# Fewer, wider products of zeros in the opening, and the second half of each pair's outputs 1.5 steps later: a gated recurrence with a squared-ReLU FFN

## The chip, the core and the metric

The kernel runs on one core of a Trainium2 chip. The core has five engines that run side by side, each with its own queue of instructions: TensorE (PE, the matrix products; its weight loads are shown as PEld), VectorE (DVE), ScalarE (ACT), GpSimd (POOL) and SyncE (SP, which here issues the transfers). Products land in eight accumulation banks (PSUM), from which DVE and ACT read them. The metric is the device time of one launch in microseconds (us); a listed time is one execution.

## The reference

A gated recurrence over 768 positions is computed for 4 batches and 8 heads of 48 elements, and its output, 3072 tokens of 384 elements, goes through a feed-forward layer with 2048 hidden elements and a squared ReLU. All of it is float32.

```python
for t in range(S):                       # S = 768
    state = alpha[:, :, t, :, None] * state + np.einsum('bhd,bhe->bhde', k[:, :, t], v[:, :, t])
    y[:, :, t] = np.einsum('bhd,bhde->bhe', q[:, :, t], state)
x = y.transpose(0, 2, 1, 3).reshape(B * S, H * D)
h = np.maximum(x @ w_in, 0.0)            # 384 -> 2048
return h * h @ w_out                     # 2048 -> 384
```

## The kernel before

*The recurrence in blocks.* The sequence is cut into 6 chunks of 128 positions; a chunk of one batch is a block, 24 in all, numbered so that four neighbours are the four batches of one chunk. A block goes through: logarithm of alpha (`ln`), running sums of it by a product with a triangle of ones (`cs`, lines 283 to 287), their exponentials (`eb`, `ei`), scaled q and k and their transposes (`turn`, tile T, line 578), and then, on PE, `scores` (line 413) and `state_sums` (line 442), both into tiles called sckv, and the outputs y (line 393). DVE takes the masked scores from the bank (`masked`, tile am) and the sums (`sums_copied`, tile us), and then makes the next state s (`next_state`).

*Pairs.* Blocks are taken in pairs. `ga` (line 502) does scores, state sums and their DVE work for a block n of the next pair, and the first half of the products of y for the pair a before: those with the state, and the inner ones on the diagonal. `gb` (line 524) does the rest of y, 32 small inner products, and then the scores, state sums and DVE work of block n + 1. After `gb` the outputs are ready: 12 copies (`ev`, line 616) bring y from its two banks to x, the input of the FFN; they run on ACT, apart from a few named in `evd`. The two banks of y are drawn in `ga` and are free once these copies have read them.

*The FFN.* Tokens are taken in six groups of four blocks. Group 0 multiplies in plain float32. From group 1 on, operands are split in parts, and three products stand for one: with parts (xa, wb), (xl, wl) and (xd, wd) in the first layer, line 726, 128x512 each, three matmuls per part; with (ha or hx), hl, hd and wb, wl, wd in the second, line 809, 128x384. ACT and DVE finish the h tiles (lines 741 to 767: `hid`, `h`), split them (lines 701 and 653) and add the parts (line 648). Group 1 still does a part of the second layer as plain products (o<-w_out,hid).

*One ring of banks.* `ps_att` and `ps_ffn` are one pool with eight banks, drawn in turn: h, o, cs, T, sckv, y, warm and zeros all draw from it, and a draw waits until the last readers of the bank drawn eight draws ago have ended.

*Who sets the order.* The program order is written by hand through the table `AT`. The opening is a list of words, `AT['first']`, each of which calls one step (line 977); among them are `warm0`, `zeros4` and `zeros1`, products of zeros whose results nobody reads: they keep PE at work while data are under way. Three more (`warm`, line 236) stand ahead of the list. After the opening, `layer_in` and `layer_out` give the units of the FFN with costs in units of about 1.2 us (an `in_x` is 1.05, an `out_x` 1.08, an `out_plain` 1), and `attention` gives events with a time on the same scale; `weave` (line 1051) puts each event ahead of the first unit whose time is not less than the event's. `attention` takes `ga` and `gb` at `t + AT['ga']` and `t + AT['gb']` where its scale is 1: that is in group 1 (for the pair that starts block 10, at t = 13, and the pair that starts block 12, at t = 35.25) and in groups 2, 3 and 4 (`AT['g']`: t = 2.075 and 14.25). With the event `gb` go the four steps of the copies (`ev_part`, at 0.1 apart) and the loads of v for the next pair and one of k, issued by SP. The splits of x for the next group stand at 51.0 (group 1) and 48.75 (the others).

The events of `attention` that matter here:

```python
w = t + (AT[f] if scale == 1 and f in ("ga", "gb") else at) * scale
...
elif f == "gb":
    if whole_at is None:
        out.append((w, gb, given))
    if after:
        for p in range(NP):
            out.append((w + AT["evs" if scale == 1 else "evs0"] * p, ev_part, (old, p)))
```

The functions that the change touches, and what calls them:

Of the kernel before, what the change touches and what calls it, by code (L numbers as in the profile page):

```python
# [9 lines left out]
FP32 = mybir.dt.float32  # L10
# [8 lines left out]


GB = 4
AT = {'thrp': 4.5, 'cvo': 3.35, 'thr': 2.25, 'm48': 16, 'cvs': 3.9, 'cv1': 0.125, 'later': (0, 0, 4, 6, 0, 1, 0), 'evs': 0.1, 'lead': 4, 'post': 3, 'w_first': (46.0, 38.0, 49.0), 'wstep': 1.0, 'w_in_at': 2.5, 'w_in_by': 3.6, 'room1': 22, 'room': 24, 's0': 4, 'ahead': 6, 'late': 2, 'xs': 0.0, 'g0': ((0.5, 4, False, True, 27.75), (25.75, 6, True, True), (29.25, 8, True, False)), 'sc0': (3.25, 2.35, 2.35), 'g1': ((5.5, 8, False, 15.0), (13.0, 10, True), (35.25, 12, True)), 'g': ((2.075, 6, True), (14.25, 8, True)), 'g1x': 51.0, 'gx': 48.75, 'g0x': 56.25, 'k0': 2, 'h0': 15, 'k1': 4, 'h1': 3, 'h1by': 2, 'evs0': 0.7, 'tp': 'ADMD', 'tp1': 'ADAD', 'split': 8, 'o0': (46.5, 48.5), 'o1': (), 'o2': (21.25, 24.75, 24.5, 40.0, 35.25, 28.25), 'str1': 21.5, 'ga': 9.75, 'gb': 12.5, 'cv0': -1.25, 'pre': '1a 0a 0q 0k 1k 1q', 'cp': ('q2a', 'k2b', 'k0a', 'k3a', 'k3b', 'k0b', 'q0b', 'q3b', 'q2b', 'q3a'), 'evd': ((0, 0, 0), (0, 0, 1), (0, 1, 2), (0, 1, 3), (2, 0, 3), (2, 1, 1), (2, 1, 2)), 'first': 'ln0 load1v cs0 ei0 eb0 zeros4 mk0 mq0 qT0 kT0 ln1 cs1 kc0 ei1 warm0 load0v eb1 mk1 qc0 weights0 lt1 sc0 load2a mq1 load2q kT1 kc1 qT1 load2k load3a qc1 load3k kv0 am0 first0 load3v sc1 ln2 kv1 load3q us0 am1 weights6 us1 cs2 ya0 ei2 second0 eb2 lt0 ln3 yb0 load2v mq2 qT2 mk2 load4a ep00 ep01 qc2 kT2 cs3 kc2 eb3 ei3 zeros1 sc2 ep02 mq3 mk3 kT3 ep03 weights2 first1 st0 ha0 second1 lt2 kv2 am2 qT3 load4k kc3 qc3 ha1 weights5 first2 sc3 kv3 am3 load4q us2 ha2 us3 ya2 yb2 weights3 ep20 ep21 ep22 load4v ep23 second2 first3 weights1 st1 weights4 ha3 lt3 hb0 st2 second3 hb2 hb3 hb1 st3'}


RUN = {0: 128, 32: 32, 64: 64, 96: 32}
# [3 lines left out]
def kernel(  # L29
# [12 lines left out]
    nc = tc.nc  # L42
# [3 lines left out]
    NP = H // 2  # L46
# [12 lines left out]
    ps_att = ctx.enter_context(tc.tile_pool(name="ps_att", bufs=8, space=PSUM))  # L59
# [11 lines left out]
    s_t = [s_all.pop(0) for _ in range(B)]  # L71
# [36 lines left out]
    def move(us, out, in_):  # L108
        ins = nc.sync.dma_start(out=out, in_=in_).ins
        ahead = 0.0  # L110
        for before, took in reversed(under_way):
            if ahead >= AT["thrp" if us == 1.0 else "thr"]:
                tc.add_manual_dep(
# [16 lines left out]
    def load(n, xs="aqkv"):  # L130
        c, b = divmod(n, B)
        for x in xs:
            t = tile_of(x, n)
            if id(t) in owner:
                need(("free", *owner[id(t)]))
            owner[id(t)] = x, n
            given.add((x, n))
            move(
                1.1,
                out=t[:, :, 0:D] if x in "qk" else t.rearrange("a (h d) -> a h d", h=H),  # L140
                in_=srcs[x][b, :, c * C : (c + 1) * C, :].rearrange("h s d -> s h d"),
            )
# [3 lines left out]
    def load_weights(i):  # L146
        src, k = (moe_w_in, KM) if i < NW else (moe_w_out, NJ // NW)
        p = i % NW * DF // NW
        src = src[:, p : p + DF // NW] if i < NW else src[p : p + DF // NW, :]
        if src.dtype == FP32:  # L150
            raws[i] = to = target(i)
            src = src.rearrange("(k r) f -> r k f", r=128)
        else:
            src = src.bitcast(U16).rearrange("(k r) f -> r k f", r=128)[:, :, 1:]
            raws[i] = raw_pool.tile([128, k, src.shape[2] + 1], U16, tag="raw", name="raw")
            to = raws[i][:, :, :-1]
        move(2.3, out=to, in_=src)
# [42 lines left out]

    for word in AT["pre"].split():
        load(int(word[0]), word[1:])
# [30 lines left out]
    nc.vector.memset(rebias, -8.0 * 14336.0)  # L233


    def warm(_):
        nc.tensor.matmul(
            out=ps_att.tile([128, NP, 64], FP32, tag="att", name="warm"),
            lhsT=s_t[0].rearrange("a p d -> a (p d)")[:, 0:128], rhs=s_t[0], start=True, stop=True,
        )  # L240

    for _ in range(3):
        warm(0)


    blk = [{} for _ in range(NBLK)]
# [4 lines left out]
    def bank(n, name, shape=(NP, C)):  # L251

        return ps_att.tile([128, *shape], FP32, tag="att", name=name)

    def work(name, bufs=1):
        return p2.tile([128, NP, C], FP32, tag=name, name=name, bufs=bufs)
# [7 lines left out]

    SPLIT = AT["split"]

# [98 lines left out]
    def copied(x, n):  # L365
        t = blk[n][f"{x}s"] = work(f"{x}s", 2 if x == "k" else 4)
        copy = nc.vector.tensor_copy if f"{x}{n}" in AT["cp"] else nc.scalar.copy
        copy(out=t, in_=blk[n].pop(f"{x}T"))
# [4 lines left out]
    def kc(n):  # L373
        (copied if n < GB else turned_copied)("k", n)


    def zeros(n):

        ps = bank(n, "zeros", (2 * NP, 64))
        for _ in range(n):  # L380
            nc.tensor.matmul(
                out=ps[:, 0 : NP // 2, :], lhsT=s_t[3].rearrange("a p d -> a (p d)")[:, 0:128],
                rhs=s_t[3][:, 0 : NP // 2], start=True, stop=True,
            )

    def y_begin(n):
        ys, seen = [bank(n, "y", (2, NP // 2, C)) for _ in range(2)], set()
# [45 lines left out]
    def state_sums(n):  # L433
        need(("v", n), ("kb", n))
        given.add(("free", "k", n))
        ps = two[n]
        m = D if n >= AT["m48"] else 64
        for p in range(NP):
# [25 lines left out]
    def rows_of(n):  # L464
        return [slice(0, D), slice(64, 64 + D)] if n >= AT["m48"] else [slice(0, 128)]

# [174 lines left out]
    here, todo, room = {}, [], [22]  # L641
# [8 lines left out]
    late = [False]  # L650
# [303 lines left out]
    steps = {f.__name__: f for f in (ln, sp, cs, eb, ei, mq, mk, bl, br, lt, qT, qc, kT, kc, ev)}  # L954
# [2 lines left out]
    steps["ya"], steps["yb"] = lambda n: ga(n, None), lambda n: gb(n, None)  # L957
    steps["load"] = load
    steps["weights"] = lambda _: load_weights(to_load.pop(0))
    steps["warm"] = warm  # L960

    def ep(n, p):
        need(*[("xp", n, i) for i in range(p)])
# [1 line left out]
        ev(n, (p,))  # L965

    steps["ep"] = ep
    steps["zeros"] = zeros

    def half_in(x, j):  # L970
        given.add(("h" + x, j))
# [5 lines left out]
    first = AT["first"]  # L977
# [129 lines left out]
    cv0 = AT["cv0"]  # L1107
    cvs = AT["cvs"]
# [17 lines left out]
    for g in range(1, NG):  # L1126
# [11 lines left out]
        if g == 1:  # L1138
# [5 lines left out]
            n = min(AT["k0"], AT["k1"])  # L1144
# [34 lines left out]
```

## Time and profile before

| | |
|---|---|
| three runs | 518.58, 518.98, 520.09 us (median 518.98) |
| span of the profiled execution | 518.6 us (its own listed time isn't given apart from these runs) |
| PE busy | 507.8 us, 5338 matmuls and as many weight loads |
| PE idle after 37 us | 1.1 us at 239 us and 0.1 at 271 us |
| DVE, ACT, POOL busy | 355.7, 306.4, 5.3 us |
| stretch 0 to 37 us | PE busy 30.9 us, DVE 20.6, ACT 24.7 |
| stretch 37 to 126 us | PE busy 88.96 us of 89.0 |
| stretch 214 to 295 us | PE busy 79.8 us of 81.0 |
| granted clock in the records | 1.00 in every stretch |
| DMA moved | 102.3 MB, 197 GB/s over the span |

The stretches are time from the span's start: the opening up to 37 us, then group 0 (to 126 us), group 1 (to 214), group 2 (to 295), group 3 (to 374), group 4 (to 449) and group 5. A busy PE is one whose records cover the time; the records of matmuls that follow each other overlap a little. What an engine waited for is inferred from semaphore events, and "issue" stands for no visible releaser. A product in float32 whose operands are not split takes two passes and appears as two matmuls.

### The profile page before, as it was taken

Reading aid. Unit: us, or ns where it says so; the run is one execution under the profiler, and the core shown is the slowest. Engines: PE = TensorE matmul, PEld = TensorE weight load, DVE = VectorE, ACT = ScalarE, POOL = GpSimd, SP = SyncE. Lnnn points to the kernel's source line nnn. Section 1 sums busy time; section 2 is a strip of 40 time slices with the busy share of each in tenths; the row PEclk is TensorE's granted clock in tenths of the full one; section 3 lists DMA queues with packets and bytes.
Section 4 is the critical chain, followed back from the end, with each engine's and each line's share of the span. In section 5 each row is a group of like instructions: output and inputs, shape, how many; then the busy total and the mean of one; then the engine's idle time right before and its main releaser. Section 6 shows DMA issues by size and latency. Waiting matters only on the chain.

```text
span 518.6 us, 13019 instructions
## 1 busy us (share of the span) xinstructions
PE 507.8 (98%) x5338; PEld 418.9 (81%) x5338; DVE 355.7 (69%) x628; ACT 306.4 (59%) x649; POOL 5.3 (1%) x29
## 2 busy tenths in 40 slices
PE   7899999999999999999999999999999999999997
PEld 5675455678888669987899988899988899988997
DVE  2766669986887877776697468587465487363861
ACT  4788898547888653485664276772275673164620
POOL 4000000000000000000000000000000000000000
PEclk9999999999999999999999999999999999999999
DMA  9999779472777786898884688864683545699201
GB/s 183 204 267 237 197 189 235 93 228 80 238 190 184 246 243 162 265 279 227 205 225 143 222 247 222 223 200 152 213 274 124 185 121 154 207 380 322 65 2 61
DMA packets 139323, 102.34 MB, mean 197 GB/s; under 512 B 109808, under 2 KB 115968, under 8 KB 139264
## 3 DMA queue, kind: packets, MB, share of 16 engines
q1 hardware_dynamic: 139264, 101.51, 68.2%
q8 instruction: 42, 0.69, 0.6%
q14 instruction: 17, 0.14, 0.1%
HBM read 84.16 MB, written 17.33 MB: 196 GB/s over the span
## 4 chain that ended last, share of the span: by engine, by line
PE 93%; DVE 4%; issue 1%; POOL 1%; ACT 1%; DVEq 0%; POOLq 0%
PE o L809 39%; PE h L726 32%; PE h L919 8%; PE y L393 4%; PE sckv L413 2%; PE T L578 2%; PE sckv L442 2%; PE cs L283 1%; PE cs L286 1%; DVE x L616 1%; PE cs L287 1%; DVE hd L648 1%; DVE hx L653 0%; DVE am L424 0%; ACT x L616 0%
## 5 line engine op out<-in xcount | busy, mean ns | idle before, releaser
L726 PE MATMUL h<-xd,wd 128*128 128x512 f32 x240 | 68.1, 396 | 1.1 <-issue 1.1
L726 PE MATMUL h<-xa,wb 128*128 128x512 f32 x240 | 68.7, 394 | 0.0
L726 PE MATMUL h<-xl,wl 128*128 128x512 f32 x240 | 67.9, 391 | 0.0
L648 DVE TENSOR_TENSOR hid<-h,hid 128x512 f32<-128x512 f32 x40 | 27.6, 689 | 51.1 <-PE h L726 51.0
L616 ACT COPY x<-y 48x256 f32<-48x256 f32 (+3 forms) x133 | 46.7, 365 | 21.2 <-PE y L393 18.8
L809 PE MATMUL o<-wb,ha 128*128 128x384 f32 x160 | 54.5, 340 | 0.0
L743 ACT ACTIVATE h<-h 128x512 f32<-128x512 f32 x40 | 23.3, 582 | 52.3 <-PE h L726 52.3
L809 PE MATMUL o<-wl,hl 128*128 128x384 f32 x160 | 53.7, 336 | 0.1
L809 PE MATMUL o<-wd,hd 128*128 128x384 f32 x304 | 53.7, 334 | 0.0
L809 PE MATMUL o<-w_out,hid 128*128 128x384 f32 x160 | 53.6, 489 | 0.0
L726 PEld LDWEIGHTS h<-xl,wl 128*128 128x128 f32 x240 | 45.1, 188 | 10.1 <-DVE xl L653 0.4
L809 PEld LDWEIGHTS o<-wd,hd 128*128 128x128 f32 x304 | 52.8, 188 | 0.0
L726 PEld LDWEIGHTS h<-xa,wb 128*128 128x128 f32 x240 | 44.4, 188 | 9.8 <-ACT hid L763 0.4
L726 PEld LDWEIGHTS h<-xd,wd 128*128 128x128 f32 x240 | 44.0, 188 | 9.1
L809 PE MATMUL o<-wb,hx 128*128 128x384 f32 x144 | 48.3, 336 | 0.0
L809 PE MATMUL o<-wl,hx 128*128 128x384 f32 x144 | 48.1, 334 | 0.0
L809 PEld LDWEIGHTS o<-w_out,hid 128*128 128x128 f32 x160 | 30.0, 190 | 19.7
L741 ACT ACTIVATE hid<-h 128x512 f32<-128x512 f32 x40 | 24.2, 606 | 32.9 <-PE h L726 32.5
L919 PE MATMUL h<-x,w_in 128*128 128x512 f32 (+1 forms) x120 | 43.4, 512 | 0.2 <-DVE x L616 0.2
L701 ACT ACTIVATE ha<-hid 128x512 fp32r<-128x512 f32 x40 | 25.1, 642 | 20.3 <-PE o L809 7.9
L919 PEld LDWEIGHTS h<-x,w_in 128*128 128x128 f32 x120 | 22.1, 190 | 17.8 <-issue 15.3
L653 DVE SCALAR_TENSOR_TENSOR hl<-ha,hid 128x512 fp32r<-128x512 f32 x40 | 27.5, 687 | 6.9 <-ACT ha L701 6.8
(111 smaller groups left out, 852.5 us busy)
## 6 DMA issues: line engine op xcount, KB each, us to landing
wd<-do SPq DMA_DIRECT2D x36, 384.0 KB
wl<-lo SPq DMA_DIRECT2D x34, 384.0 KB
wl<-li SPq DMA_DIRECT2D x32, 384.0 KB
wd<-di SPq DMA_DIRECT2D x32, 384.0 KB
raw<-in_moe_w_out_dram SPq DMA_DIRECT2D x8, 767.5 KB
raw<-in_moe_w_in_dram SPq DMA_DIRECT2D x8, 767.2 KB
v_in<-in_v_dram SPq DMA_DIRECT2D x24, 192.0 KB
out_dram<-osb SPq DMA_DIRECT2D x24, 192.0 KB
```

The lines of the kernel that those rows point to most:

```text
L393: ins = nc.tensor.matmul(out=ys[e][64 * half : 64 * half + D + G * e, m % 2, p // 2, t], lhsT=lhsT, rhs=rhs, start=(half, e) not in seen, ...
L413: nc.tensor.matmul(out=ps[e][HALF[h], 0, p, :], lhsT=ks[rows, p, HALF[h]], rhs=qs[rows, p, HALF[h]], start=True, stop=True, skip_group_che ...
L442: nc.tensor.matmul(out=ps[h][64 * e : 64 * e + m, 1, p, G:64], lhsT=tile_of("k", n)[HALF[h], 2 * p + e, 0:m], rhs=tiles["v"][n % NV][HALF[ ...
L616: copy(out=x[kk][to : to + m, t : t + 2], in_=blk[n]["y"][e][r : r + m, :, p // 2],)
L648: nc.vector.tensor_tensor(out=o, in0=x, in1=z, op=op)
L653: nc.vector.scalar_tensor_tensor(out=o, in0=x, scalar=c, in1=y, op0=ALU.mult, op1=op)
L701: nc.scalar.activation(out=a, in_=x, func=AF.Copy, scale=NEAR * E)
L726: nc.tensor.matmul(out=acc["h", j], lhsT=here[w, "i", p][:, kk, jj * 128 : (jj + 1) * 128], rhs=x_parts[x][:, kk], start=start and kk == 0 ...
L741: nc.scalar.activation(out=hid[j], in_=x, func=AF.Copy, scale=E)
L743: nc.scalar.activation(out=x, in_=x, func=AF.Copy, scale=1.0 + E)
L809: nc.tensor.matmul(out=acc[t][:, 0:DM], lhsT=lhs[:, t * C : (t + 1) * C], rhs=rhs, start=start, stop=stop, skip_group_check=True,)
L919: nc.tensor.matmul(out=ps, lhsT=w[:, kk, c0 : c0 + 128], rhs=xT[g][kk][:, cols], start=(kk == 0), stop=(kk == KM - 1),)
```

## The change

Two edits. The first is in the opening. The products of zeros that run ahead of the list of steps go from three, each 128x256 from the zeroed state tile, to two, each 128x512, whose right-hand side is one 64-element row of that tile, broadcast. In the list, `zeros4` (four products of 128x128 into one bank) gives way to one `warm0` of the new width, and two entries go: the old `warm0` after `ei1`, and `zeros1` before `sc2`. That makes three products where there were nine, and since each is two passes, each with its weight load, 24 TensorE instructions less. The function `zeros` goes.

The second edit is one number: `AT['gb']` goes from 12.5 to 14.0. The event `gb`, the four `ev_part` and the loads that go with it come 1.5 units later for eight pairs: two in each of the groups 1 to 4. `ga` stays at 9.75.

```diff
-AT = {... 'ga': 9.75, 'gb': 12.5, ...
+AT = {... 'ga': 9.75, 'gb': 14.0, ...
 'first':
-'ln0 load1v cs0 ei0 eb0 zeros4 mk0 mq0 qT0 kT0 ln1 cs1 kc0 ei1 warm0 load0v eb1 ...
+'ln0 load1v cs0 ei0 eb0 warm0 mk0 mq0 qT0 kT0 ln1 cs1 kc0 ei1 load0v eb1 ...
-... cs3 kc2 eb3 ei3 zeros1 sc2 ep02 ...
+... cs3 kc2 eb3 ei3 sc2 ep02 ...
-    def warm(_):
+    def warm(z):
         nc.tensor.matmul(
-            out=ps_att.tile([128, NP, 64], FP32, tag="att", name="warm"),
-            lhsT=s_t[0].rearrange("a p d -> a (p d)")[:, 0:128], rhs=s_t[0], start=True, stop=True,
+            out=ps_att.tile([128, 2 * NP, 64], FP32, tag="att", name="warm"),
+            lhsT=z.rearrange("a p d -> a (p d)")[:, 0:128],
+            rhs=z[:, 0:1, :].to_broadcast([128, 2 * NP, 64]), start=True, stop=True,
         )
-    for _ in range(3):
-        warm(0)
+    for _ in range(2):
+        warm(s_t[0])
-    def zeros(n):
-        ps = bank(n, "zeros", (2 * NP, 64))
-        for _ in range(n):
-            nc.tensor.matmul(
-                out=ps[:, 0 : NP // 2, :], lhsT=s_t[3].rearrange("a p d -> a (p d)")[:, 0:128],
-                rhs=s_t[3][:, 0 : NP // 2], start=True, stop=True,
-            )
-    steps["warm"] = warm
+    steps["warm"] = lambda _: warm(s_t[3])
-    steps["zeros"] = zeros
```

In the order that results, the moved `gb` stands behind more PE work than before: 2 and 16 matmuls of the second layer in group 1 (first and second pair), 9 matmuls of h in the first pair of groups 2, 3 and 4, and 8 of o in their second pair. On ACT the 12 copies stand behind activations of h that followed them or stood among them; on DVE `masked` of block n + 1 stands behind an addition of h (first pairs) or the splits and differences of h (second pairs); on SP the loads of v come one to three places later. POOL's order is unchanged.

More of the change, by code (lines that the diff above doesn't have):

```diff
@@ L21 @@
 GB = 4
-AT = {'thrp': 4.5, 'cvo': 3.35, 'thr': 2.25, 'm48': 16, 'cvs': 3.9, 'cv1': 0.125, 'later': (0, 0, 4, 6, 0, 1, 0), 'evs': 0.1, 'lead': 4, 'post': 3, 'w_first': (46.0, 38.0, 49.0), 'wstep': 1.0, 'w_in_at': 2.5, 'w_in_by': 3.6, 'room1': 22, 'room': 24, 's0': 4, 'ahead': 6, 'late': 2, 'xs': 0.0, 'g0': ((0.5, 4, False, True, 27.75), (25.75, 6, True, True), (29.25, 8, True, False)), 'sc0': (3.25, 2.35, 2.35), 'g1': ((5.5, 8, False, 15.0), (13.0, 10, True), (35.25, 12, True)), 'g': ((2.075, 6, True), (14.25, 8, True)), 'g1x': 51.0, 'gx': 48.75, 'g0x': 56.25, 'k0': 2, 'h0': 15, 'k1': 4, 'h1': 3, 'h1by': 2, 'evs0': 0.7, 'tp': 'ADMD', 'tp1': 'ADAD', 'split': 8, 'o0': (46.5, 48.5), 'o1': (), 'o2': (21.25, 24.75, 24.5, 40.0, 35.25, 28.25), 'str1': 21.5, 'ga': 9.75, 'gb': 12.5, 'cv0': -1.25, 'pre': '1a 0a 0q 0k 1k 1q', 'cp': ('q2a', 'k2b', 'k0a', 'k3a', 'k3b', 'k0b', 'q0b', 'q3b', 'q2b', 'q3a'), 'evd': ((0, 0, 0), (0, 0, 1), (0, 1, 2), (0, 1, 3), (2, 0, 3), (2, 1, 1), (2, 1, 2)), 'first': 'ln0 load1v cs0 ei0 eb0 zeros4 mk0 mq0 qT0 kT0 ln1 cs1 kc0 ei1 warm0 load0v eb1 mk1 qc0 weights0 lt1 sc0 load2a mq1 load2q kT1 kc1 qT1 load2k load3a qc1 load3k kv0 am0 first0 load3v sc1 ln2 kv1 load3q us0 am1 weights6 us1 cs2 ya0 ei2 second0 eb2 lt0 ln3 yb0 load2v mq2 qT2 mk2 load4a ep00 ep01 qc2 kT2 cs3 kc2 eb3 ei3 zeros1 sc2 ep02 mq3 mk3 kT3 ep03 weights2 first1 st0 ha0 second1 lt2 kv2 am2 qT3 load4k kc3 qc3 ha1 weights5 first2 sc3 kv3 am3 load4q us2 ha2 us3 ya2 yb2 weights3 ep20 ep21 ep22 load4v ep23 second2 first3 weights1 st1 weights4 ha3 lt3 hb0 st2 second3 hb2 hb3 hb1 st3'}
@@ new lines @@
+AT = {'thrp': 4.5, 'cvo': 3.35, 'thr': 2.25, 'm48': 16, 'cvs': 3.9, 'cv1': 0.125, 'later': (0, 0, 4, 6, 0, 1, 0), 'evs': 0.1, 'lead': 4, 'post': 3, 'w_first': (46.0, 38.0, 49.0), 'wstep': 1.0, 'w_in_at': 2.5, 'w_in_by': 3.6, 'room1': 22, 'room': 24, 's0': 4, 'ahead': 6, 'late': 2, 'xs': 0.0, 'g0': ((0.5, 4, False, True, 27.75), (25.75, 6, True, True), (29.25, 8, True, False)), 'sc0': (3.25, 2.35, 2.35), 'g1': ((5.5, 8, False, 15.0), (13.0, 10, True), (35.25, 12, True)), 'g': ((2.075, 6, True), (14.25, 8, True)), 'g1x': 51.0, 'gx': 48.75, 'g0x': 56.25, 'k0': 2, 'h0': 15, 'k1': 4, 'h1': 3, 'h1by': 2, 'evs0': 0.7, 'tp': 'ADMD', 'tp1': 'ADAD', 'split': 8, 'o0': (46.5, 48.5), 'o1': (), 'o2': (21.25, 24.75, 24.5, 40.0, 35.25, 28.25), 'str1': 21.5, 'ga': 9.75, 'gb': 14.0, 'cv0': -1.25, 'pre': '1a 0a 0q 0k 1k 1q', 'cp': ('q2a', 'k2b', 'k0a', 'k3a', 'k3b', 'k0b', 'q0b', 'q3b', 'q2b', 'q3a'), 'evd': ((0, 0, 0), (0, 0, 1), (0, 1, 2), (0, 1, 3), (2, 0, 3), (2, 1, 1), (2, 1, 2)), 'first': 'ln0 load1v cs0 ei0 eb0 warm0 mk0 mq0 qT0 kT0 ln1 cs1 kc0 ei1 load0v eb1 mk1 qc0 weights0 lt1 sc0 load2a mq1 load2q kT1 kc1 qT1 load2k load3a qc1 load3k kv0 am0 first0 load3v sc1 ln2 kv1 load3q us0 am1 weights6 us1 cs2 ya0 ei2 second0 eb2 lt0 ln3 yb0 load2v mq2 qT2 mk2 load4a ep00 ep01 qc2 kT2 cs3 kc2 eb3 ei3 sc2 ep02 mq3 mk3 kT3 ep03 weights2 first1 st0 ha0 second1 lt2 kv2 am2 qT3 load4k kc3 qc3 ha1 weights5 first2 sc3 kv3 am3 load4q us2 ha2 us3 ya2 yb2 weights3 ep20 ep21 ep22 load4v ep23 second2 first3 weights1 st1 weights4 ha3 lt3 hb0 st2 second3 hb2 hb3 hb1 st3'}
```

## The prediction

> **What bounds the kernel now.** I read, in this order, the page's busy times and its chain, the waits of PE after the opening, the tiles of the opening, and the order of time around two places that the change touches.
>
> ```profile
> span 518.6 us, 13019 instructions
> PE 507.8 (98%) x5338; PEld 418.9 (81%) x5338; DVE 355.7 (69%) x628; ACT 306.4 (59%) x649; POOL 5.3 (1%) x29
> ...
> q8 instruction: 42, 0.69, 0.6%
> ...
> PE 93%; DVE 4%; issue 1%; POOL 1%; ACT 1%; DVEq 0%; POOLq 0%
> ...
> PE h L726 <- issue: 1.1, 1, 1.1
> PE h L919 <- DVE x L616: 0.2, 1, 0.2
> ```
>
> The last two lines are all the waits of PE from 37 us to the end. So PE, after an opening that the DVE chain sets (16 to 24 us), runs without a gap but one: 1.1 us with the releaser "issue", which means that nothing the profile shows held it. The change removes no product behind the opening, hence it can help only through the opening or that gap, and can hurt wherever it makes PE wait. 518.6 is the span of the profiled execution; the shown runs are 518.58, 518.98 and 520.09, so I take span and time as equal within 0.4 us and put my sum on the median 518.98. A change under 0.3% (1.56 us: 517.4 to 520.5) can't be told from none.
>
> **The opening.**
>
> ```profile
> L237 PE MATMUL warm<-s x8: 379/634/796, 1.1 to 11.2; 128*128 128x256 f32 x8
> L381 PE MATMUL zeros<-s x10: 273/421/422, 7.1 to 22.4; 128*128 128x128 f32 x10
> 5.67 1.62 PE L283 MATMUL cs<-a_in,causal_r 128*128 128x384 f32 x2 [1.64 <-POOL us L226]
> ```
>
> Each product appears as two matmuls (two passes). The first three warm products are six passes of 256 columns at a pitch of 0.427 us, from 1.10 to about 4.0 us; two products of 512 columns are four passes of 0.853 and end at about 4.7. The cumulative sums after them start at 5.67 whatever PE does (third line: 1.64 us of waiting). Cost 0, cover 1.0 us. Eight zeros passes of 128 columns (8 x 0.213 = 1.71 us) become two of 512 (2 x 0.853 = 1.71): 0. The warm0 behind ei1 (two passes, 0.43 us at 10.99) stood inside a wait of 0.53 us for ACT's b, and zeros1 (0.22 us at 22.3) before scores that wait for ACT's ks: taking them out only lengthens these waits. Sum of the opening 0; bounds: +0.2 if the clock fell for want of the last two, and -1.0 by the next paragraph's rival.
>
> The row that could speak against this is the clock. Passes of 256 columns take 634 ns early and 379 at 11 us, and cs of 384 columns 847, later 488: half speed until about 9.9 us. The Trainium skill, "TensorE: Matmul & The Clock Gate", Part 1: The HAM clock gate, says that full speed follows a free-running window of about 3.4 us in which PE is busy; by it the longer block (3.6 us against 2.9) could bring full speed a window earlier. No row here shows that; by the pass lengths it would shorten 1.6 to 2.2 us of half-speed work (cs, zeros) by half, -0.8 to -1.1 us. I take 0 and keep it as a rival.
>
> **The one gap and the instruction blocks.** Queue q8 moved 42 packets for 10,834 PE instructions, one per 258: about every 256 instructions PE's code comes in as a 16 KB packet.
>
> ```profile
> 237.35 0.62 PE L726 MATMUL h<-xd,wd 128*128 128x512 f32 x2
> ...
> 239.08 0.40 PE L726 MATMUL h<-xd,wd 128*128 128x512 f32 x1 [1.11 <-issue]
> 239.40 0.56 PEld L393 LDWEIGHTS y<-am,v_in 64*48 64x48 f32 x32 [1.63 <-issue]
> ...
> 240.16 2.16 ACT L616 COPY x<-y 32x256 f32<-32x256 f32 x6 [2.00 <-PE y L393]
> ```
>
> The gap stands at PE instruction 5570, 62 short of 22 x 256. The packet that goes with it started 3.9 us after its boundary (1.9 to 2.2 is usual) and landed at 237.7; PE went on 1.35 us later. ga before it (320 small instructions in 2.5 us) had brought PE quickly through the block, but with a usual start the packet would have been in time. In every other place a boundary's packet landed at least 1.9 us before the next boundary came and no gap shows. With 24 instructions less, each boundary falls 24 instructions later in the work. Laying the new order over the old starts: boundary 22 moves to 240.3, and its block would be ready at 239.25 even with the same late start: -1.27. Three others fall into ga bursts, which hold a whole block: at 107.3 (next boundary 109.1), at 312.6 (314.3), and at 391.4. With a usual start (1.9), the usual 0.95 of transfer and the 1.35, the code is short by 1.0, 0.9 and 0.2 us: +2.1. Bounds: 0, if PE takes code more than one block ahead in these places, to 2.7 + 2.6 + 1.2 = 6.5 us, if the packets start as late as the one at 236.8 (1.7 us more for the first two, 1.0 for the third). I take 2.1, the usual start, which most of the 42 packets show.
>
> The Trainium skill says the opposite: "Runtime: NRT & Kernel Launch", section Instruction fetch mechanics, holds that fetching is hidden, since instructions are dispatched slower than blocks arrive, and gives PE room for eight blocks. By that rule the three stalls are nothing and the sum is 2.1 lower. The gap at 237.7 to 239.1, beside a packet, speaks against it, but only once.
>
> **The outputs 1.5 units later.** gb moves for eight pairs (groups 1 to 4, two each): behind 2 and 16 out products in group 1, behind 9 matmuls of h in the first pair of groups 2, 3, 4, behind 8 o matmuls in the second. DVE's am of the second block then stands behind one addition of h (0.69 us), ACT's 12 copies behind activations of h, and the v loads one to three places back in SP's queue; those land 10 us or more before they are used (a load issued at 246.99 serves a product at 263.45), weights likewise: 0. Nothing on POOL moves. What costs is the order of banks: two y banks are held until the copies are done.
>
> ```profile
> 322.48 0.53 PEld L726 LDWEIGHTS h<-xa,wb 128*128 128x128 f32 x3 [0.22 <-ACT hid L763]
> ...
> 322.93 2.18 ACT L616 COPY x<-y 32x256 f32<-32x256 f32 x6
> ...
> 324.34 0.34 PE L286 MATMUL cs<-hi,causal_r 128*128 128x384 f32 x1
> ...
> 325.39 0.85 PE L726 MATMUL h<-xa,wb 128*128 128x512 f32 x3
> ```
>
> - Group 2, first pair. Copies start 0.75 after the y group (239.40 to 240.16). In the new order nine come first (9 x 0.385 = 3.4), an activation of h (0.5), and the tenth (0.38) frees the first bank: y + 5.0. PE asks for that bank after y 0.49, scores and sums 0.93, two h triples 1.38, cs 0.70 and a third triple 0.69, with 0.15 for the last to drain: y + 4.3. Stall 0.7; bounds 0 (if ACT takes the copies without the activation) and 1.3 (a second activation of 0.6 between).
> - Group 3, first pair. cs at 323.99 and 324.34 takes banks that DVE's us and s must have read; before, these were 1.93 and 1.50 us early. Nine matmuls are 2.06 us, which leaves -0.13 and -0.56, and the addition ahead of am takes up to 0.69 more: 0.56 to 1.25, I take 0.7. The copies' bank is then late no further. In group 2 the same slack was 2.4, so 0; in group 4 no cs follows: 0, at most 0.4.
> - Second pairs. Here ha's split now comes ahead of the copies, which should take away the waits at 271 (0.26 and 0.09 on weight loads): -0.35; bounds -0.35 to +0.3.
> - End of group 1. The copies end at 212.1 and the last xl at 214.67, wanted at 215.24: 0.57 us of slack where 3.4 were. 0; up to +0.7 if ACT meets one more activation of 0.6 with a wait.
>
> **Sum.** 0 - 1.3 + 2.1 + 0.7 + 0.7 - 0.35 = +1.85 us, so 518.98 + 1.85 = 520.8.
>
> **Rivals.**
> - *Hidden (no change).* The fetch of code costs in no new place and the gap goes: -1.3; the bank waits come as above, +1.05: 518.7. For it: 41 of 42 packets hid. Against: none of them had a ga burst for its next block.
> - *Faster.* Gap gone (-1.3), waits of the second pairs gone (-0.35), ACT's copies in time so that no bank is waited for, and at least some of the earlier clock (-0.4 of 0.8 to 1.1): 516.9. For it: the gap is PE's one true loss behind the opening. Against: 5.0 against 4.3 and 1.5 against 2.06 are plain sums of rows.
> - *Much slower.* Packets start as late as at 236.8 also in the bursts. This decides from the point where a packet starts over 2 us behind its boundary with the DMA engines full: 4.4 us more at most, half of it likely, 523.0. For it: the DMA engines were busy at 0.72 to 0.78 in those stretches, as at 236 us. Against: the usual start.
> - *It doesn't do what it says.* The zeros products cover the same columns, so the opening may be untouched: that is already my 0, and moves no time.
>
> **Chances.** Forecast 0.37 (520.8), much slower 0.15, hidden 0.24, faster 0.24. The forecast lies just beyond 520.5, so some of it counts as same and some of hidden's upper end as slower, about alike: slower 0.50, same 0.25, faster 0.25. The likeliest one's own range, 0 to 4 us of new stalls less the gap, is 519.3 to 522.5; to hold 8 in 10 it reaches down to the faster rival, 516.7, and up to the much slower, 523.2.
>
> **What would show it.** Right: the "issue" gap at 239 gone, and new "issue" gaps of 0.2 to 1.3 us in or right behind scores and y at about 107, 313 and 391; a wait of about 0.7 for ACT's x<-y or an activation near 243, and for DVE's us or s near 324. Wrong, if PE's idle time behind 37 us stays at 1.2 us or less (then hidden or faster holds), if cs starts later than 5.7 or kT is done earlier than 10.3 (the opening did move), or if a wait over 1 us shows at 214.

## The result and the profile after

The changed kernel is slower: 522.37 us median of six runs (521.43 to 524.88) against 518.60 of six runs of the kernel before (518.04 to 520.09). The ratio is 1.0072, 95% interval 1.0052 to 1.0092, so 2.7 to 4.8 us. The forecast was 520.8, in a range of 516.7 to 523.2. A few runs of most kernels here have a granted clock of 0.990 to 0.997 and take 1.7 to 4.8 us longer than the median of the kernel's other runs; the ratios count them, so where ratios and medians disagree the medians are the better guide.

These are the head of the page of the changed kernel and its chain. Its lines stand 8 or 9 lower than those of before from line 390 on: h L726 is now L718, y L393 is L385, x L616 is L608.

```profile
span 520.3 us, 12997 instructions
PE 507.2 (97%) x5326; PEld 415.4 (80%) x5326; DVE 356.0 (68%) x628; ACT 307.6 (59%) x649; POOL 5.3 (1%) x29
...
PE 90%; DVE 5%; DMA 2%; ACT 2%; issue 1%; SPq 0%; DVEq 0%; POOLq 0%
```

And these are the waits of PE that the view lists from 37 us to the end (what waited, for what, total, times, longest); the one of h L911 still belongs to the opening, at 36.6 us, as the one of h L919 before:

```profile
PE h L718 <- DMA wd<-di: 1.0, 1, 1.0
PE y L385 <- issue: 0.5, 1, 0.5
PE h L718 <- ACT x L608: 0.5, 1, 0.5
PE h L911 <- DVE x L608: 0.2, 1, 0.2
PE cs L287 <- DVE s L469: 0.2, 1, 0.2
```

Where one gap stood, there are four: a transfer at 224 us, the copies of y at 246, code at 166, DVE's state sums at 325. PE's busy time is the same within 0.6 us, so what is lost is lost in when PE may start. Because the order of the FFN's matmuls is the same, the k-th matmul of h or o can be set beside the k-th of the other trace. Its start moves from place to place by:

| stretch of the span | start of the same matmul, after less before | step |
|---|---|---|
| end of the opening, 38 us | -0.48 us | -0.48 |
| over the code gap at 166 us | +0.28 | +0.75 |
| over the wait for wd at 224 us | +1.47 | +1.24 |
| over the gap of before at 239 us | +0.16 | -1.31 |
| over the wait for the copies at 246 us | +0.94 | +0.78 |
| over the products of y at 316 us | +1.09 | +0.14 |
| over the wait for DVE's sums at 325 us | +1.70 | +0.61 |
| over a bank of y at 327 us | +1.84 | +0.14 |
| to the end | +1.74 | -0.10 |

What is left over are -0.04 between 166 and 214 us and +0.01 near 271. Right ahead of the wait for DVE's sums the difference is +1.00, so that wait by itself is worth 0.70. The steps are larger than the idle times of the page (1.24 against 0.97 at 224): products in a row start 0.23 us apart though each lasts 0.39, and at a stop this overlap is lost.

*How typical the two profiled executions are.* The six runs of the changed kernel have time and span side by side: 522.13 and 520.3, 524.88 and 523.1, 521.43 and 519.7, and so on. A time is the span plus 1.7 to 1.8 us in all six. So the profiled span of before, 518.6, belongs to a time of about 520.4, above its highest listed run of 520.09 and 1.8 above its median. The sums are therefore consistent: 1.74 between the two profiled executions, 1.8 by which that of before was slow, and 0.24 by which that of after (522.13) was below its median, make 3.78, and 3.77 was measured. This proves little, since the 1.8 was itself taken from the difference of span and time; only the 1.74 is followed place by place.

### The profile page after: what moved, and what is told of

Read it like the earlier page. It is cut to its first block, busy times and chain, and to the rows that moved or that the text cites. A ratio compares the mean times of both kernels' runs of the same rounds, so it can differ in the third digit from the quotient of the medians.

```text
span 520.3 us, 12997 instructions
## 1 busy us (share of the span) xinstructions
PE 507.2 (97%) x5326; PEld 415.4 (80%) x5326; DVE 356.0 (68%) x628; ACT 307.6 (59%) x649; POOL 5.3 (1%) x29
## 4 chain that ended last, share of the span: by engine, by line
PE 90%; DVE 5%; DMA 2%; ACT 2%; issue 1%; SPq 0%; DVEq 0%; POOLq 0%
PE o L801 39%; PE h L718 31%; PE h L911 8%; PE y L385 4%; PE sckv L405 2%; PE T L570 2%; PE sckv L434 2%; ACT x L608 1%; DMA k_in<-in_k_dram 1%; DMA wd<-di 1%; PE cs L284 1%; DVE hd L640 1%; DVE am L416 1%; DVE hx L645 0%; PE cs L287 0%
## 5 line engine op out<-in xcount | busy, mean ns | idle before, releaser
L718 PE MATMUL h<-xa,wb 128*128 128x512 f32 x240 | 68.8, 394 | 0.5 <-ACT x L608 0.5
L718 PE MATMUL h<-xd,wd 128*128 128x512 f32 x240 | 68.1, 396 | 1.0 <-DMA wd<-di 1.0
L718 PE MATMUL h<-xl,wl 128*128 128x512 f32 x240 | 67.9, 391 | 0.0
L608 ACT COPY x<-y 48x256 f32<-48x256 f32 (+3 forms) x133 | 47.3, 365 | 24.2 <-PE y L385 21.8
L718 PEld LDWEIGHTS h<-xl,wl 128*128 128x128 f32 x240 | 45.1, 188 | 10.0 <-DVE xl L645 0.4
L718 PEld LDWEIGHTS h<-xa,wb 128*128 128x128 f32 x240 | 44.4, 188 | 10.6 <-ACT x L608 1.2
L718 PEld LDWEIGHTS h<-xd,wd 128*128 128x128 f32 x240 | 44.0, 188 | 10.3 <-ACT hid L759 1.4
L911 PE MATMUL h<-x,w_in 128*128 128x512 f32 (+1 forms) x120 | 43.3, 512 | 0.2 <-DVE x L608 0.2
L911 PEld LDWEIGHTS h<-x,w_in 128*128 128x128 f32 x120 | 22.1, 190 | 17.8 <-issue 15.1
```

The costliest lines, as they stand in the source:

```text
L608: copy(out=x[kk][to : to + m, t : t + 2], in_=blk[n]["y"][e][r : r + m, :, p // 2],)
L718: nc.tensor.matmul(out=acc["h", j], lhsT=here[w, "i", p][:, kk, jj * 128 : (jj + 1) * 128], rhs=x_parts[x][:, kk], start=start and kk == 0 ...
L911: nc.tensor.matmul(out=ps, lhsT=w[:, kk, c0 : c0 + 128], rhs=xT[g][kk][:, cols], start=(kk == 0), stop=(kk == KM - 1),)
```

## The experiments

All ratios are to the kernel before, timed on the same chip in the same series. Kernels of one series share their chip: the first four, the next four, the last four.

**The opening alone**, and **gb alone.**

```diff
 # e1_opening: open/after with
-'gb': 14.0
+'gb': 12.5
 # e2_gb14: the kernel before with
-'gb': 12.5
+'gb': 14.0
```

> The new opening alone, gb back at 12.5. Theory: the opening reaches full clock about 4.7 us into the span instead of 9.9 and ends 0.5 us earlier, and nothing else changes but the places of the instruction blocks: 0.2 to 0.8 us below the kernel before, and no wait for a wd transfer at 224 us. Rival: the 24 instructions less are what costs, by new waits for code (releaser issue): at least 0.5 us above the kernel before, with such gaps in the ga bursts.

> Only gb at 14.0, the old opening. Theory: all of the loss is in gb (1.2 us wait for wd at 224 us, 0.8 for copies of y at 246, 0.9 for DVE's state sums at 325), less nothing: 2.9 to 4.5 us above the kernel before, half clock until about 9.9 us. Rival, code blocks: the 0.5 us issue gap at 166 us is gone, and the loss is under 2 us.

The opening alone took 520.11 us against 519.21: ratio 1.0030 (1.0006 to 1.0053). It is not the gain that was expected but a loss, 0.90 us by the medians; the rival holds. gb alone took 522.18: 1.0047 (1.0028 to 1.0065), which is 1.5 to 3.4 us and meets the expected 2.9 to 4.5 only at its upper end; by the medians it is 2.97, just inside. The gap at 166 us is gone there, as the rival of that run said, but the loss isn't under 2 us by the medians. The two add up to 1.0077, and 1.0072 was measured for both.

PE's waits from 36 us on, first in the opening alone:

```profile
PE y L385 <- issue: 0.4, 2, 0.2
PE h L911 <- DVE x L608: 0.2, 1, 0.2
```

and then with gb alone:

```profile
PE h L726 <- DMA wd<-di: 1.5, 1, 1.5
PE h L726 <- ACT x L616: 0.5, 1, 0.5
PE h L919 <- DVE x L616: 0.2, 1, 0.2
PE h L726 <- issue: 0.2, 1, 0.2
PE cs L286 <- DVE s L477: 0.2, 1, 0.2
PE o L809 <- issue: 0.2, 1, 0.2
```

The three waits for wd, for x and for s come with gb, whatever the opening is. Without it, only gaps of "issue" are left behind the opening. In the second kernel the gap at 239 us, where the instructions still stand as before, was 0.18 us and not 1.1.

**gb late everywhere but in the second pair of group 1**, and **late in the first pairs of groups 2 to 4 alone.**

```diff
+    def GB_AT(n0):
+        return 12.5 if n0 in (12,) else 14.0             # e3_g1second_old
+        return 14.0 if n0 in (14, 18, 22) else 12.5      # e5_first_pairs
...
-                w = t + (AT[f] if scale == 1 and f in ("ga", "gb") else at) * scale
+                w = t + (GB_AT(n0) if scale == 1 and f == "gb" else AT[f] if scale == 1 and f == "ga" else at) * scale
```

> The changed kernel with gb at 12.5 for one pair only, the second of group 1 (the one that starts block 12); the other seven at 14.0. Theory: DVE's split of x again comes before 212 us, the output stores are issued near 214 us, SP isn't held up and wd lands in time: 1.0 to 1.5 us below the changed kernel, no wait for wd at 224. Rival: the wait for wd comes from something else, the time is within 0.4 us of the changed kernel.

> The new opening, and gb at 14.0 for the first pairs of groups 2, 3 and 4 alone, 12.5 for the five others. Theory: -0.5 of the opening, +0.8 by the copies at 246, +0.9 by the state sums at 325, nothing in group 4: 0.8 to 1.6 us above the kernel before. Rival: first pairs cost nothing when PE's instruction blocks fall elsewhere, at most 0.2 us above.

The first took 520.70 us, 1.0037 (1.0021 to 1.0054), 0.35% below the changed kernel's ratio, about 1.8 us and more than the expected 1.0 to 1.5; no wait for wd is in its trace. The second took 520.70 too, 1.0036 (1.0016 to 1.0055): inside the expected 0.8 to 1.6 above the kernel before, but only 0.6 us above the opening alone by the medians. In its trace the starts rose over the two places by 0.77 and 1.5 us (a code gap of 0.32 at 315 stands in the latter); from the end of the opening to the end of the kernel they rose by 0.91, where those of the opening alone rose by 0.08. So the waits of the first pairs are there as the theory said, but they cost 0.6 to 0.8 us net and not their sum, since the trace of the opening alone has some 0.4 us of code gap at 165 and 0.5 at 239 that this one doesn't have. Single runs of one kernel lie up to 6 us apart in that series.

**The same places in the instruction blocks.** Six products of zeros with 8 columns, 24 instructions, bring every PE instruction behind the opening back to the place it had in its block of 256.

```diff
+    def pad(n):
+        ps = bank(n, "pad", (2 * NP, 64))
+        for _ in range(n):
+            nc.tensor.matmul(
+                out=ps[0:8, 0, 0:8], lhsT=s_t[3][:, 0, 0:8], rhs=s_t[3][:, 0, 0:8], start=True, stop=True,
+            )
+    steps["pad"] = pad
-... kc0 ei1 load0v ...
+... kc0 ei1 pad6 load0v ...
 # e7_opening_padded: with gb 12.5; e8_all_padded: with gb 14.0
```

> The new opening with gb at 12.5, and six products of zeros of 8 columns (24 TensorE instructions) put behind ei1, in the wait for ACT's b, so that every later instruction stands at the place in its 256-instruction block that it had before. Theory (places in the blocks): the issue gaps that the opening alone showed at 165 and 315 us (+0.44 and +0.47 in the starts that follow) are gone, the earlier full clock stays: 0.3 to 1.0 us below the kernel before, 0.6 to 1.5 below the opening alone. Rival (noise, or the clock): the padding changes nothing, time within 0.3 us of the opening alone.

> The changed kernel with the same padding of 24 narrow instructions. Theory: 0.4 to 1.0 us below the changed kernel; the waits for wd at 224, the copies at 246 and DVE at 325 stay. Rival: the code stalls only move to other bursts, as gb stands elsewhere now: within 0.3 us of the changed kernel.

The padded opening took 518.48 us against 518.88: 0.9986 (0.9971 to 1.0001). The opening without padding had been at 1.0030, and the intervals (from 1.0006; to 1.0001) don't meet. Padded, the opening is 0.40 us ahead of the kernel before and 1.3 ahead of the opening alone by the medians, as expected, though the first of these is not beyond its interval. The padding costs nothing in its place: PE's wait for ACT's b fell from 0.96 us to 0.58. With everything changed and padded it was 521.34, 1.0046 (1.0026 to 1.0067), where gb alone had 1.0047. So the part of the loss that isn't gb's goes when the places in the blocks are restored. One profiled execution each doesn't show this: the starts end at +1.74 in the changed kernel and in its padded form. The padded one has a code gap of its own, 0.54 us at 341 us; gb alone, whose instructions behind the opening have the same places, has one of 0.17 at the same instruction (the last line of its waits). PE's waits in the padded opening:

```profile
PE h L718 <- issue: 0.3, 1, 0.3
PE sckv L434 <- issue: 0.3, 1, 0.3
PE h L911 <- DVE x L608: 0.2, 1, 0.2
```

The first is the gap of before, again at 237.2 us, with 0.28 for 1.11. The traces alone would make the padding worth only 0.4 us behind the opening (against the kernel before, the opening alone moved its starts by +0.44 at 165, -0.8 at 239 and +0.46 near 315; the padded one by -0.85 and about +0.5 at the last two). By the medians (+0.90 and -0.40 against the kernel before) it is 1.3, by the ratios 2.3, where two long runs of the opening alone (524.57 and 524.82) weigh. Code gaps differ from run to run, as the one at 239 does, and one profiled execution doesn't give their mean.

**gb late for the other four pairs.**

```diff
+    def GB_AT(n0):
+        return 14.0 if n0 in (10, 16, 20, 24) else 12.5
```

> The new opening, gb at 14.0 for the second pairs of groups 2, 3 and 4 and the first of group 1, 12.5 elsewhere. Theory: these four cost nothing and gain at most 0.1: the time of the opening alone, within 0.4 us. Rival: they carry part of the loss, 0.5 us or more above the opening alone.

519.57 us, 1.0019 (1.0005 to 1.0033), by the medians 0.69 above the kernel before where the opening alone had 0.90; these pairs cost nothing that can be seen.

**Group 1's stores not on SP.**

```diff
     def store(g, t, o):
...
+        if g == 1:
+            nc.gpsimd.dma_start(out=out[r0 : r0 + C, :], in_=o)
+            return
         move(0.5, out=out[r0 : r0 + C, :], in_=o)
```

> The changed kernel with the four pairs of output stores of group 1 issued by POOL and not by SP, everything else as changed. Theory: SP no longer stands 7 us behind DVE's last additions, wd of group 2 is issued several us earlier, the wait at 224 us is gone although gb is at 14.0 for all eight pairs: 0.8 to 1.5 us below the changed kernel. Rival: wd is late because its transfer is slow or its buffer comes free late: the wait stays, time within 0.4 us.

521.14 us, 1.0043 (1.0027 to 1.0058), about 1.5 us below the changed kernel by the ratios, as expected. Its times are the span plus 2.03 to 2.09 us, where all other kernels have 1.73 to 1.85, so another 0.3 us that it gains in the span is lost outside. Its waits of PE from 37 us:

```profile
PE h L718 <- ACT x L608: 0.5, 1, 0.5
PE y L385 <- issue: 0.4, 1, 0.4
PE cs L287 <- DVE s L469: 0.2, 1, 0.2
```

wd is gone from the list, although gb is late for all eight pairs. What held it is read off SP's queue. First the waits of the queue from 205 to 222 us in the changed kernel, then the DMA engines' busy share in 40 slices of the stretch from 209 to 225 us in the changed kernel:

```profile
SPq L109 <- DVE osb L640: 6.2, 1, 6.2
```

```profile
DMA  7998999741100000000000599957999979799999
```

and the same stretch with the stores issued by POOL:

```profile
DMA  8998998999999999999979999899999999976477
```

In the changed kernel SP stood 6.2 us before the first store of group 1's outputs (2.8 in the kernel before), and behind this store, in the same queue, stood the loads of group 2's weights. The DMA engines stood still for 4.4 us (2.0 in the kernel before); with the stores elsewhere no such hole is left. This is the timeline of the changed kernel there (start, duration, engine, line, operation, out<-in):

```profile
207.86 4.36 ACT L608 COPY x<-y 32x256 f32<-32x256 f32 x12 [10.55 <-PE y L385]
...
212.91 1.90 DVE L645 SCALAR_TENSOR_TENSOR xl<-xa,x 128x512 fp32r<-128x512 f32 x3 [2.30 <-ACT xa L693]
214.72 1.89 DVE L640 TENSOR_TENSOR xd<-xl,xa 128x512 fp32r<-128x512 f32 x3
216.53 1.95 DVE L640 TENSOR_TENSOR osb<-o,osb 128x384 f32<-128x384 f32 x4
...
217.11 1.32 SPq L109 DMA_DIRECT2D out_dram<-osb  x3
...
219.74 0.42 SPq L109 DMA_DIRECT2D wd<-di  x1
...
224.41 0.93 PE L718 MATMUL h<-xd,wd 128*128 128x512 f32 x3 [0.97 <-DMA wd<-di]
```

And these are the same steps in the kernel before:

```profile
205.24 3.97 ACT L616 COPY x<-y 32x256 f32<-32x256 f32 x11
...
213.52 1.95 DVE L648 TENSOR_TENSOR osb<-o,osb 128x384 f32<-128x384 f32 x4
...
214.09 1.82 SPq L109 DMA_DIRECT2D out_dram<-osb  x4
...
215.96 0.45 SPq L109 DMA_DIRECT2D wd<-di  x1
```

The copies come 2.6 us later than before, then the split of x, and DVE adds up the outputs only after xl and xd: osb starts at 216.53 where it had started at 213.52. The stores follow, and then the weights: the wd load that left at 215.96 leaves at 219.74, and 4.5 us later it has landed, just ahead of the product at 224.41. Each is a queue in its own order, ACT, DVE, SP, and none was the bound by itself.

**Two instruments on the opening.** The old products of 256 columns, three of them, ahead of an opening that is new in all else; without padding, and with five narrow products as padding.

```diff
 # e15_narrow_shifted and e11_narrow_padded (gb 12.5)
-    for _ in range(2):
-        warm(s_t[0])
+    for _ in range(3):
+        nc.tensor.matmul(
+            out=ps_att.tile([128, NP, 64], FP32, tag="att", name="warm"),
+            lhsT=s_t[0].rearrange("a p d -> a (p d)")[:, 0:128], rhs=s_t[0], start=True, stop=True,
+        )
 # e11_narrow_padded only
-... kc0 ei1 load0v ...
+... kc0 ei1 pad5 load0v ...
```

> The opening alone (gb 12.5), but with the three old products of 256 columns ahead of it in place of the two of 512: 20 instructions less than before. Theory (places in the instruction blocks cost, early full clock gains): the opening ends within 0.4 us of that of the kernel before with half clock until 9 us or later, the issue gaps in the ga bursts stay: 0.5 to 1.8 us above the kernel before. Rival: the wide products are what costs, and this one is within 0.3 us of the kernel before.

> The same three old products of 256 columns, and five narrow products as padding, so that no instruction behind the opening is shifted. Theory: nothing is left that differs from the kernel before behind the opening, and full clock comes late again: within 0.5 us of the kernel before, 0.3 to 0.8 us above the opening padded with the wide products. Rival: the padded opening was ahead by something else than the clock, and this one is as fast, 518.5.

The shifted one took 519.76 us against 519.74, 1.0008 (0.9988 to 1.0029); the padded one 519.46, 0.9995 (0.9979 to 1.0012). The padded one is within 0.5 us of the kernel before, as expected; whether it lies 0.3 to 0.8 us above the padded opening with wide products isn't settled (0.9986 there, the intervals overlap). The shifted one was expected 0.5 to 1.8 us above and has the median of the kernel before; its interval holds both readings. So 20 instructions less cost nothing that can be seen, though its trace too has a code gap, 0.22 us at 314; that the places cost rests on the opening alone and the four other pairs, 0.90 and 0.69 above by the medians, against the padded opening. And its expectation of a late full clock failed: with the old narrow products PE's cs took 562 ns at 5.1 us, full speed, while the kernel before, with the same first products, showed 980. What the width does to the clock is therefore not shown (see the last section).

**The two best parts together**, the padded opening and the four harmless pairs late:

```diff
+        return 14.0 if n0 in (10, 16, 20, 24) else 12.5
-... kc0 ei1 load0v ...
+... kc0 ei1 pad6 load0v ...
```

> The padded opening with gb at 14.0 only where nothing waited for it: the first pair of group 1 and the second pairs of groups 2, 3 and 4. Theory: the small waits near 271 us shrink by at most 0.2 us: the time of the padded opening, 518.0 to 518.8. Rival: it meets new waits for code as the bursts stand elsewhere, 0.5 us or more above it.

519.29 us against 519.74, 0.9991 (0.9974 to 1.0008): no more than the padded opening. (The expected 518.0 to 518.8 came from a series in which the kernel before took 518.88.) Neither it nor that opening beats the kernel before beyond its interval, if narrowly in the latter case.

**Copies on DVE.**

```diff
-'evd': ((0, 0, 0), ...
+'evd': ((12, 1, 1), (12, 1, 2), (0, 0, 0), ...
```

> The changed kernel, but two of the groups of copies of y of group 2's first pair (half 1, p 1 and 2) on DVE in place of ACT. Theory: the first y bank comes free before the activation of h and its tenth copy on ACT, the wait at 246 us goes, later starts fall by 0.5 to 0.8 us there; the other waits (224, 325) stay; 0.3 to 0.9 us below the changed kernel. Rival: DVE is later with its sums and additions and PE waits for it in place of ACT: no gain.

523.13 us, 1.0073 (1.0046 to 1.0101): no gain. The rival was right that DVE is late, but not that the wait changes its name; it grew from 0.5 to 1.1 us. The timeline of this kernel tells why:

```profile
242.16 1.52 ACT L608 COPY x<-y 32x256 f32<-32x256 f32 x4 [0.74 <-PE y L385]
...
244.82 1.32 DVE L608 COPY x<-y 64x256 f32<-64x256 f32 x3
...
245.27 0.82 ACT L608 COPY x<-y 16x256 f32<-16x256 f32 x2 [1.58 <-DVE x L608]
...
246.11 0.60 ACT L733 ACTIVATE hid<-h 128x512 f32<-128x512 f32 x1
...
246.73 1.14 ACT L608 COPY x<-y 64x256 f32<-64x256 f32 x3
...
247.15 0.96 PE L718 MATMUL h<-xa,wb 128*128 128x512 f32 x3 [1.12 <-ACT x L608]
```

DVE could begin its copies only at 244.82, behind the masked scores and the state sums, and ACT stopped 1.58 us in the middle of its row until DVE had passed. The bank came free later than with all twelve on ACT.

## Why the prediction was right, and where not

The time lies in the range, but not by the sum as it was made up. The forecast had +0.8 for opening and code (0 - 1.3 + 2.1) and +1.05 for gb. The opening alone measured +0.90 by the medians, and that it agrees is luck, since both code terms were too large. gb alone measured +2.97, and most of what is missing there is one wait that was put at 0.

**Copies of y in group 2's first pair: right, term 0.7, measured 0.78.** It was worked out that nine copies run, an activation of h comes between, and the tenth frees the bank. The changed kernel shows just that:

```profile
242.39 3.31 ACT L608 COPY x<-y 32x256 f32<-32x256 f32 x9 [0.74 <-PE y L385]
245.71 0.60 ACT L733 ACTIVATE hid<-h 128x512 f32<-128x512 f32 x1
246.32 0.75 ACT L608 COPY x<-y 64x256 f32<-64x256 f32 x2
```

The y group began at 241.64, PE asked for the bank at 246.25 and had it at 246.73. The step of starts was 0.77 to 0.79 in all traces with this pair late except that of the copies on DVE.

**DVE's sums in group 3's first pair: 0.7 taken, 0.70 measured, but the working is right only in part.** The changed kernel shows these rows:

```profile
323.64 0.77 DVE L416 COPY_PREDICATED am<-halves_mask,sckv 128x256 f32<-128x256 uint32 x2 [1.34 <-PE sckv L434]
324.31 0.73 DVE L448 TENSOR_TENSOR us<-sckv,s 48x192 f32<-48x192 f32 x2
325.08 0.74 DVE L469 TENSOR_TENSOR s<-sckv,us 48x192 f32<-48x192 f32 x2
...
325.97 0.42 PE L287 MATMUL cs<-hi,causal_r 128*128 128x384 f32 x1 [0.18 <-DVE s L469]
```

PE stops at cs until s has read its bank, as foreseen. But the addition of h that was to push am back by up to 0.69 us is done before: DVE stands idle for 1.34 us ahead of am. What is left of the sum is its 0.56, and cs starts 0.15 us behind the end of s. And "the copies' bank is then late no further" is not so: the weight load behind it waits 0.33 us for ACT's copies of x at 327.14, which moves the starts by 0.14. **Group 4** cost nothing, as said.

**Second pairs: a gain of 0.35 was foreseen, none was measured** (the step there is 0.01, and these pairs alone changed nothing).

**End of group 1: taken as 0, bounds to +0.7; 1.24 measured (1.2 to 2.0 in the four kernels with the wait).** This step failed in kind, and it is the largest error of the sum. The text looked only at when xa and xl are ready (slack 0.57, which held, no wait for them came) and said of the transfers that they land 10 us or more ahead of use, on the strength of loads that no store stands in front of; the one behind the store, issued at 215.96 in the kernel before, serves a product at 223.04, 7 us on. It didn't follow the later copies through xl and xd to DVE's last additions, from there to the stores, and from the stores to the weight loads queued behind them on SP. That the stores in SP's queue are the link is shown by the kernel that issues them elsewhere.

**Code: right in one of three places, too large, and one place missed.** The prediction foresaw new gaps at 107, 313 and 391 us worth 2.1 and the end of the one at 239, worth -1.27. No trace has a gap at 107 or 391. Near 315, where 0.9 had been put, seven of the eight kernels with unpadded openings show gaps of 0.17 to 0.53 (0.4 to 0.8 in the starts that follow), at the same instruction within two; the changed kernel's starts rise there by 0.14; and none of the six kernels with the old places has one there (the padded opening has one at 318.8, 254 instructions on). At 166 one of 0.5 (a step of 0.75) wasn't foreseen, and the one at 239 was gone in the changed kernel. What held is the mechanism: gaps with the releaser "issue" end shortly behind the landing of a 16 KB packet on the instruction queue: 1.35 us for the gap of before, 1.45 for that at 166 (packet 162.95, took 1.44), 1.51 for that at 315 with the stores on POOL (312.35, took 1.13), 1.24 to 1.66 in all. What failed is the forecast of when packets start: around 109 us, where the text had one start, they started at 104.25, ahead of the burst, and at 110.15. How much the places cost was measured by the padding, though in two series: 1.3 us by the medians. The padding brings the gap at 239 back too, so this is to be set beside 2.1 - 1.27 = 0.8.

**The opening: taken as 0, measured -0.48 in the profiled execution.** The prediction's own signs of being wrong came: cs started at 5.77, later than 5.7, and kT was done at 9.80, before 10.3. The rival's clock did come early there: cs at 5.77 us took 562 ns and the one after it 486, where before they took 980 and 847, and kT began at 9.20 instead of 9.83. The Trainium skill, "TensorE: Matmul & The Clock Gate", Part 1: The HAM clock gate, gives a free-running window; a switch that moves from run to run, as below, agrees with that.

**The starting point: the other step that failed.** The text set the span of 518.6 equal to the time within 0.4 us, and took -1.27 for the gap at 239. But time is span plus 1.8, the profiled execution was 1.8 us above the median, and the gap of 1.11 is mostly its own: at that very place five kernels with the instructions as before (everything changed and padded, gb alone, the padded opening, the narrow padded one, the two best parts) show none, 0.18, 0.28, 0.28 and 0.51. So some 0.6 to 1.1 of it was credit for something that other executions don't lose. Between the two profiled executions the sum of +1.85 stands beside 1.74; against the medians 3.77 was measured. The rest of the 1.8 is not explained here; the opening, which ends up to 1.1 us earlier in other kernels' traces, is one candidate.

Of the full loss, gb has 0.47% (0.28 to 0.65) and the opening 0.30% (0.06 to 0.53). Within gb, group 1's second pair has 1.2 to 2.0 us by the traces (1.5 and 1.8 by ratios of the two kernels without its wait), the first pairs of groups 2 and 3 about 1.6 by the steps in the changed kernel's trace, but 0.6 by the medians of the run that has them alone.

**Rivals.** That the loss would be hidden fell; so did "faster". "Much slower", with late packets, came near the time (523.0) for another reason: not packets of code, but the wait for wd.

## What to carry to other kernels

When work moves later, follow it through every queue that is in order: what stands behind it on its engine, which transfer waits for that, and what stands behind that transfer on the issuing queue; a store that waits blocks each load behind it. Before a gap in a profile is booked as a possible gain, ask whether the profiled execution is a typical one: compare its time (not its span) with the median. And where the tensor engine issues hundreds of small instructions, removing instructions elsewhere moves the places at which code is fetched; here that went with 0.7 to 0.9 us, and padding to the old count is a way to compare without it.

## What was not expected of the hardware

The clock. The granted clock reads 1.00 in every stretch, but early passes take twice as long, and the switch wanders: with the two wide products first, full speed came between 4.1 and 7.2 us in nine traces and after 9 us in one; with the three narrow ones at 5.2, about 8.9 and twice about 9.9 us. The wide ones may help, but four traces against ten, and a narrow one as early as the wide, don't settle it. The rows are PE's passes: warm of 512 columns 1061 ns and then 592, cs 980 and then 486 to 562.

The fetch of code. The Trainium skill, "Runtime: NRT & Kernel Launch", section Instruction fetch mechanics, has it hidden; here gaps of 0.1 to 1.1 us end 1.24 to 1.66 us behind a packet of 16 KB, in or soon behind streams that issue 320 small instructions in 2.5 us. They come back at the same few instructions from kernel to kernel, but not with the same size: one place, in six kernels that have the same instructions there, gave none, 0.18, 0.28, 0.28, 0.51 and 1.11 us.
